# Retention and maxout feed-forward on one core: another order of the first chunks, fewer identity products, weight sums of five units in tile 0

## The chip, the cores and the metric

The kernel runs on one core of a Trainium2 chip. The metric is the device time of one execution in microseconds (us). "Before" and "after" are always timed on the same chip in alternating rounds. A ratio compares the mean times of the two kernels' fast runs in the same rounds, so it isn't quite the ratio of the medians that are quoted.

## The reference

Retention (attention with a decay instead of a softmax), then a feed-forward part with a maximum of three products. All of it is float32; the weights arrive as float64.

```python
B, H, S, D = 8, 8, 576, 64
scores = (q @ k.T) / sqrt(D)              # per batch and head
ret    = scores * gamma[h] ** (i - j)     # for i >= j, else 0
x      = (ret @ v), heads side by side    # 4608 x 512
h      = maximum(maximum(x @ w1, x @ w2), x @ w3)   # 4608 x 768
out    = h @ w_out                        # 4608 x 512
```

## The kernel before

Rows go in 36 chunks of 128 (`g`) and 9 tiles of four chunks (`t`). A chunk has three steps: `transposes` (q and k by identity products on TensorE for the first eight chunks, copied out by ScalarE), `scores` (q times k, mask on VectorE, and the running state), `values` (times v and state, then a multiply into `xT`).

```python
def transposes(g):                       # first eight chunks
    for n, src in (("k", ...), ("q", ...)):
        ... nc.tensor.transpose(pt[:, p, :], pair(src, p), ident[:C, :C])
        nc.scalar.copy(t[:], pt[:])
def scores(g):
    ... nc.tensor.matmul(s[j][:, p, :], lhsT=kT..., rhs=qT...)
    ... nc.vector.tensor_tensor(st[:, j], s[j][:], mask, op=ALU.mult)
    ... nc.tensor.matmul(kv...)
    ... nc.vector.tensor_tensor(t[:], kv[:], states[g][:], op=ALU.add)
        nc.gpsimd.tensor_tensor(t[:], t[:], gs[:], op=ALU.mult)
def values(g):
    ... nc.tensor.matmul(o...)           # st times v, then state times q
    nc.vector.tensor_tensor(xT[t][:, :, i * C:(i + 1) * C], o[:], gq[:], op=ALU.mult)
```

In the traces each engine takes its instructions in the order in which they are written (after the change, for example, ScalarE's copies for chunk 3 come at 23.40 us, behind its steps for the first weight piece, which are written ahead of them). The float64 weights are taken apart by hand, 24 pieces of 128x512; `convert(n)` does the next n of about four steps of a piece. The steps as they fall on the engines (V = VectorE, A = ScalarE, G = GpSimd, which the profile calls DVE, ACT and POOL; there PE is TensorE and PEld its loading of weights):

```python
V expo = high & mask          A mant = low * 2**-52 + 1          # step 1
A expo = relu(...)  V frac = high & 0xFFFFF  A expo = relu(...)  # step 2
V mant = frac * 2**-20 + mant                                    # "whole"
V expo = sign | expo          G w = mant * expo                  # "product"
```

Tile 0 multiplies plainly (`up_plain`, eight matmul records per piece of weights). Later tiles use a scheme of seven smaller products in place of eight (`up`), which needs sums of weight blocks for each of nine units (a unit is one of `w1`, `w2`, `w3` with one of three pairs of column blocks), made once:

```python
def weight_sums(n):
    nc.vector.tensor_tensor(t1, b12, b11, op=ALU.subtract)
    nc.vector.tensor_tensor(t2, b22, t1, op=ALU.subtract)
    nc.gpsimd.tensor_tensor(b12, b22, b12, op=ALU.subtract)
    nc.gpsimd.tensor_tensor(t4, b21, t2, op=ALU.subtract)
```

`sums_of_outs` does the same for the output weights, as small "chores" during `up`. `warm(n)` issues n products of the identity with itself, which count for nothing but keep TensorE busy.

## Time and profile before

| | |
|---|---|
| time | 836.27 us, median of 3 runs (836.2 to 837.62) |
| span of the profile | 834.5 us |
| TensorE busy | 825.3 us |
| first feed-forward product starts | 31.63 us |
| second weight piece used from | 35.13 us |
| pauses of TensorE in tile 1 against its usual step | 0.90 us at 161.63, 0.98 us at 184.25 |

The page, the waits, the chain and the timeline of this kernel are shown and read in the prediction below. In the chain's lines the first number is the start, the second the length (us), then the engine and the source line. In a timeline's lines the bracket tells how long the engine had been idle and what ended it.

### The profile page before, as it was taken

The page shows a single profiled execution, that of the slowest core. Times are in us where ns is not written, and L with a number is a line of the kernel's source. Part 1 is how long each engine was busy: PE and PEld are TensorE (multiplying, and loading weights), DVE is VectorE, ACT ScalarE, POOL GpSimd, SP SyncE. Part 2 cuts the span into 40 slices and gives each one's busy share as a digit, 9 for nine tenths or more (in the row PEclk, how much of TensorE's full clock was granted, in tenths as well). Part 3 has the DMA queues.
Part 4 walks back from the last instruction along what each step waited for, and adds up shares of the span by engine and source line. Part 5 has one row for each costly group of instructions (what it writes and reads, how often), then busy time and mean ns, then how long its engine had stood idle before and what let it go on. Part 6 is the DMA issues. An engine that isn't in the chain of part 4 may idle for free.

```text
span 834.5 us, 12656 instructions
## 1 busy us (share of the span) xinstructions
PE 825.3 (99%) x4636; PEld 671.3 (80%) x4636; DVE 425.9 (51%) x803; ACT 175.1 (21%) x395; POOL 186.9 (22%) x182
## 2 busy tenths in 40 slices
PE   9899999999999999999999999999999999999998
PEld 8555556878888888888888888888888888888887
DVE  2979934774354543554454544544544435433341
ACT  2656721111111101111111111111111011111211
POOL 3435523362211130212011121111111202201000
PEclk9999999999999999999999999999999999999999
DMA  9946521333123322332233313332332224201001
GB/s 225 258 151 188 134 57 42 55 58 75 56 54 57 57 58 58 74 56 56 58 56 67 74 50 55 57 57 81 56 57 54 59 52 79 48 13 38 1 1 50
DMA packets 232509, 59.06 MB, mean 71 GB/s; under 512 B 213504, under 2 KB 230912, under 8 KB 232448
## 3 DMA queue, kind: packets, MB, share of 16 engines
q1 hardware_dynamic: 232304, 58.26, 31.0%
q8 instruction: 36, 0.59, 0.3%
q14 instruction: 25, 0.20, 0.1%
q10 hardware_dynamic: 144, 0.00, 0.0%
HBM read 48.76 MB, written 9.44 MB: 70 GB/s over the span
## 4 chain that ended last, share of the span: by engine, by line
PE 96%; SPq 1%; DVE 1%; DMA 1%; issue 0%; ACT 0%; POOL 0%; POOLq 0%; DVEq 0%
PE x L435 29%; PE z L435 14%; PE dx L311 10%; PE up L493 7%; PE y L435 7%; PE dz L311 5%; PE s L183 5%; PE o L213 4%; PE o L218 4%; PE kv L194 4%; PE dy L311 2%; PE down L484 2%; SPq L146 1%; DMA qraw<-in_q_dram 1%; PE warm L113 1%; PE kt L173 0%
## 5 line engine op out<-in xcount | busy, mean ns | idle before, releaser
L435 PE MATMUL x<-S,T 128*128 128x256 f32 x576 | 147.8, 379 | 0.0
L435 PEld LDWEIGHTS x<-S,T 128*128 128x128 f32 x576 | 109.2, 190 | 15.2
L156 POOL TENSOR_TENSOR vd<-vraw,gk 128x512 f32<-128x512 f32 x36 | 38.8, 1077 | 342.5 <-DMA vraw<-in_v_dram 333.1
L435 PE MATMUL x<-S,w 128*128 128x256 f32 x288 | 74.6, 381 | 1.6 <-DVE h L465 1.6
L435 PE MATMUL x<-xT,w 128*128 128x256 f32 x288 | 74.8, 382 | 0.0
L435 PE MATMUL y<-xT,w 128*128 128x256 f32 x288 | 73.9, 379 | 0.0
L435 PE MATMUL z<-S,w 128*128 128x256 f32 x288 | 73.9, 379 | 0.0
L435 PE MATMUL z<-xT,T 128*128 128x256 f32 x288 | 73.9, 379 | 0.0
L440 ACT COPY p<-x 128x256 f32<-128x256 f32 x72 | 26.8, 373 | 220.5 <-PE x L435 217.8
L465 DVE TENSOR_TENSOR tmp<-x,p 128x256 f32<-128x256 f32 x48 | 20.4, 425 | 103.0 <-PE x L435 103.0
L186 DVE TENSOR_TENSOR st<-s,causal 128x512 f32<-128x512 f32 x72 | 46.3, 685 | 47.9 <-PE s L183 47.9
L493 PE MATMUL up<-xT,w 128*128 128x512 f32 x144 | 63.6, 594 | 2.3 <-DVE xT L220 2.3
L435 PEld LDWEIGHTS x<-S,w 128*128 128x128 f32 x288 | 49.3, 189 | 15.4 <-DVE h L465 2.6
L220 DVE TENSOR_TENSOR xT<-o,gq 128x512 f32<-128x512 f32 x36 | 24.8, 690 | 71.7 <-PE o L218 65.7
L435 PEld LDWEIGHTS y<-xT,w 128*128 128x128 f32 x288 | 54.7, 190 | 7.4
L435 PEld LDWEIGHTS z<-S,w 128*128 128x128 f32 x288 | 54.7, 190 | 7.4
L435 PEld LDWEIGHTS z<-xT,T 128*128 128x128 f32 x288 | 54.0, 189 | 8.2
L435 PEld LDWEIGHTS x<-xT,w 128*128 128x128 f32 x288 | 51.5, 190 | 6.6 <-issue 0.8
L493 PEld LDWEIGHTS up<-xT,w 128*128 128x128 f32 x144 | 26.6, 190 | 32.9 <-issue 29.4
L294 POOL TENSOR_TENSOR H<-h 128x256 f32<-128x256 f32 x24 | 18.8, 784 | 148.2 <-DVE h L478 148.2
L440 ACT COPY u<-x 128x256 f32<-128x256 f32 x72 | 26.8, 373 | 99.9 <-PE x L435 98.5
L454 DVE TENSOR_TENSOR tmp<-y,p 128x256 f32<-128x256 f32 x48 | 20.4, 425 | 51.5 <-PE y L435 51.5
(92 smaller groups left out, 1224.7 us busy)
## 6 DMA issues: line engine op xcount, KB each, us to landing
bits<-in_moe_w_dram SPq DMA_DIRECT2D x18, 512.0 KB, 4.9
out_dram<-osb SPq DMA_DIRECT2D x36, 256.0 KB, 2.1
kraw<-in_k_dram SPq DMA_DIRECT2D x32, 256.0 KB, 3.0
vraw<-in_v_dram SPq DMA_DIRECT2D x32, 256.0 KB, 3.5
qraw<-in_q_dram SPq DMA_DIRECT2D x448, 16.0 KB, 1.8
kxraw<-in_k_dram SPq DMA_DIRECT2D x448, 16.0 KB, 1.8
bits<-in_moe_w_out_dram SPq DMA_DIRECT2D x6, 512.0 KB, 3.4
qraw<-in_q_dram SPq DMA_DIRECT2D x7, 256.0 KB, 4.5
```

Source lines behind the costliest of these rows:

```text
L156: nc.gpsimd.tensor_tensor(t[:], raws.pop(("v", g))[:], gk[:].unsqueeze(2).to_broadcast([C, H, D]), op=ALU.mult)
L183: nc.tensor.matmul(s[j][:, p, :], lhsT=kT[r, p, :], rhs=qT[r, p, :], start=True, stop=True)
L186: nc.vector.tensor_tensor(st[:, j], s[j][:], masks[start_of(g)][:].unsqueeze(1).to_broadcast([C, NP, C]), op=ALU.mult)
L194: nc.tensor.matmul(kv[:, p, :], lhsT=pair(kr, p)[r:], rhs=pair(vds[g], p)[r:], start=True, stop=True)
L213: nc.tensor.matmul(o[D * j:D * (j + 1), p, :], lhsT=vr[:, 2 * p + j, :], rhs=st[:, j, p, :], start=(p == 0), stop=(old == 0 and p == NP - ...
L218: nc.tensor.matmul(o[:, p, :old], lhsT=sd[:, p, :], rhs=qT[:, p, :old], start=False, stop=(p == NP - 1), skip_group_check=True)
L220: nc.vector.tensor_tensor(xT[t][:, :, i * C:(i + 1) * C], o[:], gq[:], op=ALU.mult)
L311: nc.tensor.matmul(out[:, m, :], lhsT=hS[n](fp)[:, m * P:(m + 1) * P], rhs=late["T"][n][:, fp, :], start=first and m == 0 and fp == 0, sto ...
L435: nc.tensor.matmul(out[:], lhsT=w[:, d * P:(d + 1) * P], rhs=xS[t][n][:, d, :], start=first and d == 0, stop=d == 1, skip_group_check=True)
L440: nc.scalar.copy(c[:], src[:])
L454: nc.vector.tensor_tensor(c11, y[:], p1[:], op=ALU.add)
L493: nc.tensor.matmul(ps[:], lhsT=w_sb[i, fb][:, dc * P:(dc + 1) * P], rhs=xT[t][:, dc, :], start=(dc == 0), stop=(dc == NDC - 1))
```

## The change

It lets a chunk's scores follow its own transposes at once, with the next chunk's transposes under the mask, so that TensorE works instead of warming itself. Weight sums move to the last products of tile 0, where VectorE and GpSimd are free, so that less of them crowds tile 1.

```diff
@@ ffn
             else:
+                if t == 1 and n == 0:
+                    sums_of_outs()
                 for _ in up(t, h, fp, i):
                     pass
                 if t == 1:
-                    weight_sums(n + 2)
+                    weight_sums(n + 5)
                 if i == 2:
-                    if t == 1 and fp == 0:
-                        sums_of_outs()
                     sums_of_hidden(h, fp)
@@ ffn, last products of tile 0
                 down(t, h, m)
-                if m >= 2:
-                    weight_sums(m - 2)
+                for n in [[0], [1], [2], [3, 4]][m]:
+                    weight_sums(n)
@@ start
-    warm(9)
+    warm(6)
     ... (loads unchanged)
     decay_values(0)
+    transposes(0)
+    warm(3)
     decay_values(1)
-    transposes(0)
-    warm(5)
+    scores(0)
     transposes(1)
+    values(0)
     decay_values(2)
-    scores(0)
-    values(0)
+    scores(1)
     transposes(2)
+    values(1)
     decay_values(3)
-    scores(1)
+    scores(2)
+    convert(2)
     transposes(3)
-    values(1)
-    scores(2)
-    convert(3)
     values(2)
+    convert(2)
+    scores(3)
     decay_values(4)
-    scores(3)
-    convert(1)
-    transposes(4)
     convert(2)
     values(3)
+    transposes(4)
     convert(4)
```

## The prediction

> **What bounds the kernel now.** I read the page first. Its first part says that TensorE is the engine that counts:
>
> ```profile
> PE 825.3 (99%) x4636; PEld 671.3 (80%) x4636; DVE 425.9 (51%) x803; ACT 175.1 (21%) x395; POOL 186.9 (22%) x182
> ```
>
> Matmul ends are modelled, so 99% could hide short pauses. I therefore compared the starts of neighbouring matmuls in the timeline with the usual step of their kind (a 128x512 one starts 0.43 us after the one before it, a 128x256 one 0.216 us). Between the first product of the feed-forward part (31.63 us) and the end, TensorE keeps that step except at two places. The view of waits for PE names them, together with the late start of the first product:
>
> ```profile
> PE up L493 <- DVE xT L220: 2.3, 1, 2.3
> PE x L435 <- DVE h L465: 1.6, 2, 0.8
> ```
>
> So what can be won without removing matmuls is the time before 31.63 us plus about 1.9 us of pauses (0.90 and 0.98 us against the usual step), at 161.63 and 184.25 us. The removed identity products, the only matmuls that go, lie at the very start.
>
> The start: the chain of waits for the first 40 us, read from its end backward.
>
> ```profile
> 6.95 1.12 PE warm L113 x10
> ...
> 12.28 4.36 DMA qraw<-in_q_dram
> 16.63 0.14 issue
> 16.77 0.63 PE qt L173 x4
> 17.40 1.02 PE o L213 x16
> ...
> 26.33 0.45 PE kt L173 x4
> 26.78 0.68 DVE state L199
> 27.46 0.60 DVE expo L381
> 28.06 1.41 DVE expo L365
> 29.47 1.41 DVE frac L370
> 30.88 0.61 DVE xT L220
> 31.49 0.14 issue
> 31.63 7.21 PE up L493 x16
> ```
>
> Three facts are in it. TensorE waits for the DMA of the fourth chunk's q until 16.63 us. Then it has 12.5 us of its own work: values 1, scores 2, values 2, scores 3, transposes 4, values 3. Last, the multiply into xT (chunk 3) stands behind four VectorE steps, mostly weight conversion, though its matmuls end at about 29.3. The windows give a DMA busy share of 0.84, 0.96 and 0.96 in the first three 10 us. The warm products end at 8.07, long before the DMA wait, so they are off this path.
>
> The rest of the start, from the timeline: the first weight piece is not there before 20.6 us, and VectorE's mask steps, usually 0.42 us, take 1.5 us when POOL is at work.
>
> ```profile
> 20.60 0.77 ACT L366 ACTIVATE mant<-bits,one 128x512 f32<-128x512 uint32 x1 [2.58 <-DMA bits<-in_moe_w_dram]
> ...
> 27.54 1.65 POOL L200 TENSOR_TENSOR state<-state,gs 128x512 f32<-128x512 f32 x1 [0.55 <-DVE state L199]
> 27.98 1.50 DVE L365 TENSOR_SCALAR expo<-bits 128x512 int32<-128x512 int32 x1
> 29.15 1.44 POOL L387 TENSOR_TENSOR w<-mant,expo 128x512 f32<-128x512 f32 x1
> 29.39 1.49 DVE L370 TENSOR_SCALAR frac<-bits 128x512 int32<-128x512 int32 x1
> ```
>
> Each of those two DVE steps ends 0.29 us after the POOL step it met (29.19 and 29.48; 30.59 and 30.88).
>
> **What the Trainium skill says.** "SBUF — State Buffer", section "Who interferes with whom": VectorE and GpSimd share a port pair, held exclusively for a whole instruction; a tensor_scalar in a two-port mode, or a DVE step with two SBUF inputs, waits while GpSimd has it. The trace agrees: the 1.50 us above, and weight sums on DVE that take 0.94 and 0.83 us beside POOL instead of 0.41. "TensorE: Matmul & The Clock Gate", section "What's actually happening": the array runs at half clock until one busy window of about 3.4 us has passed, and an idle window of that length brings it back. Here the warm products start 0.213 us apart, and the record of the granted clock goes from half to full at 6.4 us. "Perfetto Trace Analysis", section "Sequencer Loop": instructions sit in one queue per engine, and each waits for its semaphores. I use this as: a waiting head of a queue holds up everything behind it. The trace agrees (POOL's multiply of v waits 333 us in all for its DMA, and the weight sums queued behind it run only after it).
>
> **The change, part by part.**
>
> *Identity products.* 14 become 9, in records 28 become 18 (each fp32 product is two). That is 10 records of 0.213 us cold, or 0.11 warm: 1.1 to 2.1 us of TensorE. All of it lies before the DMA-paced part: worth 0. The first chunk's products, moved up, keep TensorE busy in their place, so I expect the clock to rise at about 6.4 us again.
>
> *The first chunks' order.* Estimate from durations of the timeline: transposes 0.45 us for each of k and q, scores 1.1, kv 1.1, values 1.0 (+1.1 with state), ACT copies 0.59, masks into st 1.29 per chunk, landings of the inputs as before since the issue order is unchanged. Scores 0 at 6.75, values 0 at 9.9, scores 1 at 10.9, transposes 2 at 13.1 (their inputs land at 12.2 and 13.1), values 1 at 14.0 to 16.1, scores 2 at 16.1 to 18.3, transposes 3 at 18.3, values 2 at 19.2 to 21.3. So far TensorE is 2.8 us ahead of before, where values 2 end and scores 3 start at 24.08. But now the first two conversion steps are written ahead of transposes 3. ScalarE therefore sits on the weight piece until 20.6, then does mant 0.77, expo 0.72, expo 0.72 (to 22.85), and only then the two copies of transposes 3 (to 24.05). Scores 3 start at 24.1, as before, and 2.8 us of the lead are lost in that queue.
> After that: scores and kv 3 to 26.3; st from 25.3 to 26.6; values 3 to 28.7, because transposes 4 (1.0 us) now come after them. On DVE: state 26.6 to 27.25, expo 0.42, then frac, which meets POOL's multiply of the state (27.35 to 28.65) and ends at 28.95. The whole and product steps of piece 0 are already done by 23.6, and its POOL step by 25, so the second meeting of before goes away. xT from 28.95 to 29.6, first product at about 29.7 in place of 31.63: 1.9 us. The second weight piece: whole, expo, frac, product (0.68+0.42+0.42+0.68) from 29.6, plus POOL 1.4: 33.1, and TensorE wants it at 29.7+3.5 = 33.2. It just fits (before: 0.06 us to spare).
> Does the lead survive to the first tile's end? Weight pieces 2 and later are ready 3 us or more before their product, PSUM buffers are free 9 us or more ahead, and VectorE has idle stretches of 0.9, 2.4 and 0.9 us at 47 to 57 us spent waiting for TensorE, so it can follow. Yes.
>
> *Weight sums earlier.* One unit's sums are two DVE steps of 0.42 us and two POOL steps of 0.73 us, 1.8 us on either engine when they meet. Three more units move into the last products of tile 0, where DVE is idle 5.2 us (110.34 to 115.56) and 6.5 us (117.44 to 123.92). Units 0 and 1 go there, and 2, 3, 4 after xT of chunk 7, where two stood: DVE is done with transposes and the first output sums at about 134.5 to 135.5 instead of 131.7; its next need is at 136.02. No new wait. After tile 1's units 0 to 3 follow sums of units 5 to 8; after units 4, 5 and 6 nothing. The two pauses both come from the pile on DVE after the third unit of a triple; for the second:
>
> ```profile
> 179.63 0.94 DVE L414 TENSOR_TENSOR T<-w,w 128x256 f32<-128x256 f32 x1
> ...
> 180.60 0.83 DVE L415 TENSOR_TENSOR T<-w,T 128x256 f32<-128x256 f32 x1
> 181.36 0.70 DVE L167 STREAM_TRANSPOSE kT<-kxraw 128x512 f32<-128x512 f32 x1
> ...
> 183.79 0.41 DVE L465 TENSOR_TENSOR h<-x,p 128x256 f32<-128x256 f32 x1
> ```
>
> Without the two T steps (1.77 us) the step of 183.79 runs some 1.2 us earlier or more, when its matmuls end (about 182.6), and the pause of 0.98 us is gone. The pause of 161.63 stays: the T steps of another unit stand at that place, and the output sums give way to hidden sums of like size. POOL is fuller there (two output sums and two weight sums queue behind the v multiply of 155.57), so it may grow by 0.3. Sum: 0.7 us won.
>
> *Total:* 836.27 - 1.9 - 0.7 = 833.7, rounded to 833.6.
>
> **Rivals.** (a) ScalarE's queue isn't a brake, if the first piece lands sooner or the copies get through: scores 3 at 21.5 and the first product at about 27.5; then weight pieces 0 and 1 become the bound. For it: the new order wants this. Against: the issue order is unchanged and the DMA is 0.96 busy. Time 831.5 to 832.5. (b) A DVE mask step meets POOL once more before xT (+1.4), or the second piece comes 1 us late, as the 0.06 us of before warn. The start then gives 0 to 0.5 and the time is 835.2. (c) Both pauses stay, or the fuller POOL queue makes new ones in tile 1's units 0 to 3: 1 to 2 us lost, time about 835. (d) Both pauses go, as output sums are done by unit 1: 832.7. (e) The clock falls back in TensorE's idle 21.3 to 24.1: 2.8 us is less than one window, and the 2.3 us idle of before did nothing; if so, about +1.
>
> **Range and chances.** Everything that moves lies within 31.6 us of start and 1.9 us of pauses, and the inputs' DMA fixes most of the start. Gains beyond 5 us or losses beyond 2 us need something that I don't see. Three runs before spread 1.4 us (836.2 to 837.62). I take 831.8 to 835.8. A change of 2% is 16.7 us: 0.5% for each side.
>
> **What would show it.** Right: transposes 3 on ACT wait for the first weight piece; scores 3 start near 24; first product at 29.3 to 30.2; no wait at unit 6 of tile 1, one of about 1 us at unit 3; the rest shifted unchanged. Wrong: a first product before 28.5 or after 31, a wait of TensorE between 33 and 134 us, waits in tile 1's units 0 to 2, or a clock that rises later than 7 us.

## The result, and the profile after

The changed kernel took 834.93 us (median of 4 runs, 832.89 to 835.73), the kernel before 836.24 (4 runs, 835.09 to 837.62): ratio 0.998, with an interval of 0.9957 to 1.0003, so these runs alone don't tell it from no change. The time is inside the predicted range, 1.3 us above the predicted 833.6. The profile was taken in the slowest of the four executions (835.73 us, span 834.0), so it shows a bad case, as the experiments make plain.

The page of the changed kernel, first part (busy us, share of the span, number of records):

```profile
PE 823.8 (99%) x4626; PEld 670.5 (80%) x4626; DVE 427.3 (51%) x803; ACT 174.7 (21%) x395; POOL 186.7 (22%) x182
```

The ten records of identity products are gone and TensorE is busy for 1.5 us less. Its waits (total us, times, longest us):

```profile
PE s L183 <- ACT qT L175: 2.0, 1, 2.0
...
PE up L493 <- POOL w L387: 1.4, 1, 1.4
PE x L435 <- DVE h L465: 1.2, 1, 1.2
```

One of the two pauses in tile 1 is left and has grown: against the usual step it is 1.34 us, at 162.03 us. The wait for xT is gone; in its place are a wait of the scores for ScalarE and one of the feed-forward part for a weight piece. The chain of waits at the start shows both:

```profile
14.57 5.89 DMA bits<-in_moe_w_dram
20.46 0.02 issue
20.49 1.41 DVE expo L365
...
21.92 0.73 ACT expo L368
...
22.68 0.72 ACT expo L371
23.40 0.47 ACT kT L175
23.87 0.49 ACT qT L175
...
24.41 1.21 PE s L183 x16
...
32.05 2.94 POOL w L387
34.99 0.04 issue
35.03 3.70 PE up L493 x8
```

The first weight piece lands at 20.46 us; ScalarE works on it; then come the copies of chunk 3 and its scores at 24.41. The piece's first step on VectorE takes 1.41 us where 0.42 is usual; POOL's multiply of the state runs beside it, from 20.32 to 21.60. The first feed-forward product starts at 30.00 us (before: 31.63). The lead is 1.6 us there, but the second weight piece is ready only at 34.98 us, and the second product starts at 35.03 where it started at 35.13 before. Of 1.6 us, 0.1 is left. POOL shows why. Its record for that piece is 2.93 us long (2.94 in the chain), where one such multiply alone is 1.27 (the kernel before, in its profile: 1.65). The timeline of the kernel before at its second piece (one line), then that of the changed kernel (the POOL line merges two multiplies):

```profile
33.43 1.65 POOL L387 TENSOR_TENSOR w<-mant,expo 128x512 f32<-128x512 f32 x1 [2.84 <-DVE expo L381]
```
```profile
31.88 0.69 DVE L376 SCALAR_TENSOR_TENSOR mant<-frac,mant 128x512 f32<-128x512 int32 x1
32.05 4.16 POOL L387 TENSOR_TENSOR w<-mant,expo 128x512 f32<-128x512 f32 x2 [1.92 <-DVE expo L381]
32.48 0.43 DVE L365 TENSOR_SCALAR expo<-bits 128x512 int32<-128x512 int32 x1
32.81 0.43 DVE L370 TENSOR_SCALAR frac<-bits 128x512 int32<-128x512 int32 x1
33.15 0.69 DVE L381 SCALAR_TENSOR_TENSOR expo<-bits,expo 128x512 int32<-128x512 int32 x1
```

POOL's multiply starts at 32.05, just after a VectorE step. VectorE goes on with three more without a gap, until 33.84, and POOL ends at 34.98, 1.1 us after that and 1.27 us after 33.71. So it seems to have waited through nearly four VectorE steps in a row and only then had the port pair that the two engines share ("SBUF — State Buffer" of the Trainium skill, section "Who interferes with whom").

From 35 to 134 us nothing in TensorE's steps differs between the two kernels, and the shift of 0.1 us stays. Tile 1 gives 0.5 us (0.98 gone, 0.90 grown to 1.34). The sum, 0.6 us, is close to the difference of the two profiles' spans (834.5 and 834.0). But the four times lie up to 2.8 us apart, so something at the start must differ from execution to execution. That was the first thing to test.

### The profile page after: what moved, and what is told of

It is laid out like the page before. It is cut to its first block, busy times and chain, and to the rows that moved or that the text cites. A ratio compares the mean times of both kernels' runs of the same rounds, so it can differ in the third digit from the quotient of the medians.

```text
span 834.0 us, 12632 instructions
## 1 busy us (share of the span) xinstructions
PE 823.8 (99%) x4626; PEld 670.5 (80%) x4626; DVE 427.3 (51%) x803; ACT 174.7 (21%) x395; POOL 186.7 (22%) x182
## 4 chain that ended last, share of the span: by engine, by line
PE 95%; DMA 2%; DVE 1%; SPq 1%; ACT 0%; POOL 0%; issue 0%; DVEq 0%
PE x L435 30%; PE z L435 15%; PE dx L311 10%; PE y L435 7%; PE up L493 7%; PE dz L311 5%; PE s L183 4%; PE o L213 4%; PE o L218 4%; PE kv L194 4%; PE dy L311 2%; PE down L484 2%; SPq L152 1%; DMA bits<-in_moe_w_dram 1%; DMA gs<-in_state_decay_dram 1%; SPq L146 1%
## 5 line engine op out<-in xcount | busy, mean ns | idle before, releaser
L183 PEld LDWEIGHTS s<-qT,kT 64*128 64x128 f32 x576 | 35.0, 187 | 15.6 <-issue 11.7
```

Of the source, the lines that this page charges most:

```text
L183: nc.tensor.matmul(s[j][:, p, :], lhsT=kT[r, p, :], rhs=qT[r, p, :], start=True, stop=True)
```

## The experiments

Theory A: the landing of the first weight piece paces the start through ScalarE's queue, and a race between POOL and VectorE at the second piece gives back up to 1.5 us of it. Rivals: the spread lies elsewhere (matmul rate, DMA, clock), or the order alone decides. Twelve kernels ran in three groups of four, five rounds each, each group on another chip. The kernel before had medians of 837.52, 837.79 and 837.22 us in the three groups, so kernels of different groups are compared by their ratios to it.

| run | median us | ratio to before (95% interval) | first, second product start in its profile, us |
|---|---|---|---|
| group 1: changed again | 834.69 | 0.9968 (0.9951 to 0.9986) | 28.07, 31.81 |
| new start only | 834.26 | 0.9971 (0.9952 to 0.9990) | 30.25, 33.99 |
| weight sums only | 836.64 | 0.9995 (0.9978 to 1.0012) | 31.66, 36.87 |
| second piece on VectorE | 833.24 | 0.9953 (0.9936 to 0.9970) | 29.51, 33.01 |
| group 2: before, filled | 836.58 | 0.9985 (0.9973 to 0.9998) | 31.81, 35.32 |
| changed, filled | 833.81 | 0.9952 (0.9939 to 0.9966) | 29.50, 34.55 |
| copies first | 832.32 | 0.9939 (0.9927 to 0.9951) | 28.51, 33.55 |
| skip the third unit | 833.03 | 0.9945 (0.9931 to 0.9958) | 29.99, 33.77 |
| group 3: fourteen products | 835.67 | 0.9968 (0.9952 to 0.9984) | 30.85, 35.89 |
| three edits | 830.86 | 0.9921 (0.9908 to 0.9934) | 28.22, 31.72 |
| masks first | 832.05 | 0.9933 (0.9919 to 0.9946) | 28.89, 33.16 |
| weight first | 831.41 | 0.9926 (0.9912 to 0.9939) | 28.25, 31.76 |

### The changed kernel once more

No edit.

> The changed kernel itself, once more. Theory A (in the first profile POOL lost the shared port four times in a row while it formed the second weight piece, and the second feed-forward product began at 35.03 instead of 33.4 us): executions differ by whether POOL loses that race, so the median is 0.5 to 2.2 us under before, the first product starts at 29.7 to 30.3 us in this profile too, and the second anywhere from 33.4 to 35.1. Rival B (the spread lies elsewhere, in matmul rate or DMA): the second product starts at 35.0 again, and the time is 0.5 us under before; the spread shows as a shift that grows along the whole span.

The ratio is 0.9968, or 2.7 us of the 837.5, against 0.998 in the first runs, and here the interval lies clear of 1. The profile is of a good execution (832.3 us). Two things are better in it than in the first one. The first weight piece lands at 19.22 us (20.46 in the first profile), so scores 3 start at 22.48 and the first product at 28.07. And POOL gets the port at the second piece after one VectorE step; the timeline of this run:

```profile
30.11 1.65 POOL L387 TENSOR_TENSOR w<-mant,expo 128x512 f32<-128x512 f32 x1 [1.90 <-DVE expo L381]
30.56 1.49 DVE L365 TENSOR_SCALAR expo<-bits 128x512 int32<-128x512 int32 x1
```

This time it is VectorE that waits, 1.49 us for a step of 0.42. The second product starts at 31.81, 3.74 us after the first; in the first profile it was 5.04 us after. The pause at the fourth unit of tile 1 is 1.17 us. The expectation had the first product between 29.7 and 30.3, which was too narrow: the DMA's landing moves too. Its Rival B fails: the second product did not start at 35.0 again, and the difference lies at the start.

In the seven profiles that have the changed order with ScalarE on the first piece before chunk 3's copies (the changed kernel twice, new start only, second piece on VectorE, changed and filled, skip the third unit, fourteen products), the first product starts 8.8 to 9.6 us after that piece lands, over landings from 19.22 to 22.02 us. Its start follows the landing, as Theory A says. The second product starts at 31.81 to 35.89 us in the six of them that leave the second piece to POOL, 34.2 on average, against 35.13 and 35.32 in the two profiles of the old start without a fall of the clock (see below): about 1.0 us earlier.

### Each half alone

New start only: the hunks in `ffn` undone. Weight sums only: the start's hunk undone.

```diff
 # new start only, against the changed kernel
-                    weight_sums(n + 5)
+                    weight_sums(n + 2)
 ... (sums_of_outs after the third unit, weight_sums(m - 2) after products 2 and 3 of tile 0)
```
```diff
 # weight sums only, against the changed kernel
-    warm(6)
+    warm(9)
 ... (the start in the order of before)
```

> The new order of the first chunks and the nine identity products, with the weight sums as before. Theory A: first product at 30.0 us, second at 33.4 to 35.1, the two pauses near 161 and 184 us stay (0.9 and 1.0 us): 0.1 to 1.7 us faster than before. Rival B: the order itself is worth its 1.6 us in every execution, as another first product's end hides the second piece: 1.6 us faster.

> The weight sums as changed, with the order of the first chunks and fourteen identity products as before. Theory A: first product at 31.6 us, second at 35.1, the pause after the fourth unit of tile 1 grows to 1.3 us and the one after the seventh is gone: 0.5 us faster than before. Rival C: without the new start the two pauses both go or both stay: 1.9 us faster, or 0.

The new start alone is worth 0.29% (2.4 us), the sums alone 0.05% (0.4 us, interval across 1), together 0.34% against 0.32% for the whole. Within these intervals the halves add up. In the profile of the new start the two pauses stay at 0.84 and 0.97 us. In that of the sums the seventh unit's pause is gone and the fourth's stays at 0.90, so it has not grown there. (Five of the six runs of the sums alone have the slowdown told of next, against seven of the eleven of before, so their 0.4 us may be too low.)

The profile of the sums alone shows something that no theory had. The second product comes 5.2 us after the first, although its weight piece is ready at 35.12, as before. The windows of that run (start and end, length, busy us of PE, PEld, DVE, ACT and POOL with counts, then the granted clock as a share of full speed, DMA share, GB/s):

```profile
30.00:33.00 3.00, 1.34 (x3) 0.71 (x4) 3.00 (x6) 2.15 (x4) 0.63 (x1) 0.95 0.66 233
33.00:37.00 4.00, 4.00 (x7) 1.63 (x6) 3.34 (x5) 0.93 (x2) 2.23 (x2) 0.61 0.60 174
```

The granted clock is 0.61 in the second window. The record of the clock has it at half from 32.7 to 36.1 us, for 3.4 us, and the second product starts 1.7 us later than it does after a first product in full clock (5.2 against 3.5 us). Ahead of it TensorE stood idle from 29.3 to 31.66, the wait for xT that the kernel before has too.

Why here and not in the profile of before? The clock records of the packed traces tell. In the run of the sums alone the clock rises to full at 5.40 us and falls at 32.71, eight times 3.413 us later. Counted in stretches of 3.413 us from the rise, the 14 profiles hold 15 falls (this one, and one in each after its last matmul), and every one comes at the end of a stretch. Each of these 15 stretches had 2.23 us or more without a matmul (this one 2.31); none of the other 3373 had over 1.89. In the profile of before the rise is at 6.40 us, so a stretch ends at 30.29: the same wait of 2.3 us is split into 0.98 and 1.33 us, and no fall follows. So in these traces a wait of this length costs again only when it falls almost whole into one stretch.

Each run's mean clock, which doesn't count the time before the first rise (it is 1.000 in the profile of before), tells whether such a fall took place ahead of the last matmul: 3.4 us at half speed is 0.2% of the span. The fall after the last matmul takes up to 0.1% (0.999 in five of the profiles), so I count a fall at 0.998 or less. Of the 31 runs of the kernel before in the three groups, 19 are at 0.998 or 0.997. Their medians are 837.95, 838.08 and 838.34 us, and those of the other 12 runs 835.5, 836.9 and 836.6. The changed kernel has three such runs of six in group 1 (834.9 to 835.1, the rest 832.3 to 834.5), and none of its first four. This became Theory D.

### Second weight piece on VectorE

```diff
-            nc.gpsimd.tensor_tensor(w, mant[:], expo[:].bitcast(FP32), op=ALU.mult)
+            engine = nc.vector if piece == pieces[1] else nc.gpsimd
+            engine.tensor_tensor(w, mant[:], expo[:].bitcast(FP32), op=ALU.mult)
```

> The changed kernel, but the multiply that forms the second weight piece is done by VectorE (0.68 us, estimate from its like) instead of POOL, so POOL has nothing to fetch through the shared port there. Theory A: the second piece is ready near 32.6 us, the second product starts at 33.4, no wait, and the whole is 1.5 us under the first profile of the changed kernel (span about 832.5), with less spread. Rival B (something else holds the second product, such as the queue of DVE or the landing of a piece): it starts at 34.5 or later again and the time doesn't move by over 0.3 us.

The piece is ready at 32.19 us and the second product starts 3.51 us after the first, which is its own length: no wait is left. The step in the timeline of this run:

```profile
31.50 0.69 DVE L388 TENSOR_TENSOR w<-mant,expo 128x512 f32<-128x512 f32 x1
```

The median is 1.4 us under the changed kernel's on the same chip (833.24 against 834.69), though the two intervals overlap. Only one run of six has a fall of the clock. That POOL's part, and not the landing or VectorE's queue, held the second product is shown by the profile; that POOL waited for the port is read from the times of its record, and no run isolates it.

### Filling TensorE's idle time

```diff
 # kernel before
     values(3)
+    warm(8)
     convert(4)
```
```diff
 # changed kernel
     convert(2)
+    warm(6)
     scores(3)
```

> The kernel before, with eight identity products more (16 records, 1.8 us at 0.112 us, an estimate from the warm ones of the profile of before) in TensorE's idle time of 2.3 us ahead of the first feed-forward product. Theory D (the granted clock falls to half for one window of 3.4 us, as in the profile of the sums alone from 32.7 us, when TensorE stands idle for most of a window; each fall costs 1.7 us): the runs with a mean clock of 0.998 or less, 7 of 11 for the kernel before, nearly vanish, and the median comes to 835.2, some 2 us under before. Rival E (falls are the chip's own, whatever TensorE does): the same share of runs at 0.998, and the time of before.

> The changed kernel, with six identity products (1.35 us) in TensorE's idle time before the scores of chunk 3. Theory D: no or hardly any run at 0.998, so the slow ones (834.9 to 835.1) go: median 832.5 to 834.0, against 834.7; what remains of spread is POOL's wait at the second weight piece. Rival E: half of the runs at 0.998 as before, median 834.7.

Work that counts for nothing makes the kernel before faster: ratio 0.9985, 836.58 against 837.79 us. None of its five runs is at 0.998 or less (five of nine of the kernel before in the same rounds are), and its median is 0.3 us under that of the unfallen runs of before on this chip (836.9). The expected 835.2 was taken from another chip's runs and missed. The changed kernel filled has no fall in five runs either. Its profile shows the lost race at the second piece again (5.04 us between the products), and it stays at 834 to 835 in two runs. Five runs each are few, but the whole record bears Theory D out. The profiles of the kernel before, the sums alone, the changed kernel, the new start only, second piece on VectorE, skip the third unit and fourteen products all show a wait of TensorE of 2.0 us or more between 8 and 32 us (but for the second one of the changed kernel, 0.7), and 33 of the 70 runs of these kernels that have a clock on record show a fall. In the other six kernels (the two filled ones, copies first, three edits, masks first and weight first) the longest wait there is 1.2 us, and none of 30 runs has a fall. What spread remains in the changed kernel I put down to the race and the landing. Only one fall ahead of the last matmul was ever profiled; that the other 0.998 runs have theirs at TensorE's wait of the start is inferred from these counts.

### Copies of chunk 3 first

```diff
-    convert(2)
     transposes(3)
+    convert(2)
```

> The changed kernel, with the transposes of chunk 3 written ahead of the first two conversion steps, so that their copies on ScalarE don't wait for the first weight piece. Theory A: scores 3 start at 21.5 in place of 24.4, but their masks on VectorE now queue behind the steps of the first piece (until about 24.3), so the first product comes at 28.7 (1.3 us earlier), and the second at 32.2 to 33.7. With TensorE's pause moved after the scores; 0.5 to 1.5 us faster than the changed kernel. Rival (ScalarE's queue is all that held it): first product at 27.2, 2.8 us earlier. Rival (second weight piece is the bound): first product earlier, the second at 35.0 all the same, no gain.

Scores 3 start at 21.94 us and the first product at 28.51, close to what Theory A expects. This run's first piece landed as late as 21.25, and the changed order would have given 30.0 or later (8.8 us after it). The median is 832.32; the ratio is 0.29% better than the changed kernel's in group 1, part of it because none of the five runs has a fall. But now the masks wait behind the first piece's steps on VectorE: in the chain of waits, the product step of the first piece ends at 24.20 and the masks follow. The race at the second piece was lost here as well, with 5.04 us between the products.

### No weight sums after the third unit

```diff
-                    weight_sums(n + 5)
+                    weight_sums({0: 5, 1: 6, 3: 7, 4: 8}.get(n, len(units)))
```

> The changed kernel, with the weight sums of units 5 to 8 after units 0, 1, 3 and 4 of tile 1 instead of 0, 1, 2 and 3, so none stand between the third unit's maxima and the fourth unit. Theory A (the two T steps on VectorE, 1.77 us, make the pause at the fourth unit): the pause of 1.2 to 1.3 us is gone or under 0.2 us, and nothing new at the seventh unit: 1.2 us faster than the changed kernel. Rival (POOL's queue behind the late multiply of v makes it, through the shared port): it stays at 0.6 us or more.

Both pauses are gone; TensorE keeps its step all through tile 1. VectorE reaches the step that the fourth unit waits for with time to spare, in the timeline of this run:

```profile
158.83 0.42 DVE L465 TENSOR_TENSOR h<-x,p 128x256 f32<-128x256 f32 x1 [0.62 <-PE x L435]
```

It had been idle 0.62 us and waited for TensorE, not the other way. POOL, though the edit takes two of its steps away here as well, still works without a gap from its multiply of v at 153.95 us to 163.27, so that rival falls. The ratio is 0.9945 against 0.9968 in group 1: 0.23%, with intervals that overlap. The pause, 0.91 to 1.39 us in the profiles with the changed sums and the new start, is worth some 0.14%.

### Fourteen identity products

```diff
-    warm(6)
+    warm(9)
 ...
-    warm(3)
+    warm(5)
```

> The changed kernel with all fourteen identity products back (nine, then five). Theory A: the first scores start about 0.9 us later, but the scores of chunk 1 wait for the state decay's DMA (landing at 10.1 to 11.1 us) and those of chunk 3 for the first weight piece, so it is caught up: first product at 28.0 to 30.3 as in the changed kernel's profiles, time within 0.5 us of 834.7 to 834.9. Rival (fewer identity products are worth their 1.1 to 2.1 us): first product 1 to 2 us later and the time by as much longer.

The ratio is 0.9968, the same as with nine. With intervals of 1.4 us to either side the times alone could not exclude the rival's 1.1 us; the profile does. In it scores 0 start at 8.29 us instead of 7.17, scores 1 at 12.37 instead of 11.99, and scores 3 at 25.26, which is 3.24 us after the first piece's landing (22.02 in this run), as in the good run with nine (3.26). So 1.1 us at chunk 0 is 0.4 at chunk 1 and nothing at chunk 3. The removed products were worth nothing by themselves. The expected bound of 30.3 us for the first product missed (30.85), because the piece landed later than in any other profile.

### Three edits at once

Copies first, second piece on VectorE, and no sums after the third unit, as shown above.

> The changed kernel with three edits at once: the copies of chunk 3 first, the second weight piece formed on VectorE, and the sums skipped after the third unit. If their causes are separate, the gains add: first product at 28.5, second at 32.0, no pause in tile 1: 1.3 to 1.5 us (start), 1.2 (POOL's lost races, in about half of the executions), 1.2 (pause): median 831.0, against 834.7. If they share a cause, it comes to 832.0 or more, as the copies first alone (832.3).

The gains add: 830.86 us, ratio 0.9921, the best, 6.4 us under the kernel before on the same chip. Its five runs lie within 1.5 us, none has a fall of the clock (seven of the eleven of before on this chip have one, so a part of the gain is that). In the profile the products start at 28.22 and 31.72 us, and these are all the waits of TensorE that the view lists:

```profile
PE warm L113 <- POOL ident masks.py:199: 1.4, 1, 1.4
PE o L213 <- DVE st L186: 0.6, 2, 0.4
```

The first is the wait for the identity at the very start, the second the masks of chunk 3.

### Masks of chunk 3 first

```diff
     transposes(3)
     convert(2)
     values(2)
-    convert(2)
     scores(3)
-    decay_values(4)
-    convert(2)
+    convert(2)
     values(3)
+    decay_values(4)
+    convert(2)
     transposes(4)
     convert(4)
```

> As the three edits, and the scores and masks of chunk 3 are written ahead of the last two steps of the first weight piece, and values 3 ahead of the second piece's first two steps. Theory A (in the copies-first kernel VectorE's queue took over from ScalarE's, as the wait of values 3 for st shows): first product at 27.6, second at 31.1: 0.9 us faster than the three edits, median 830.1. Rival: the first weight piece on POOL is now late (27.5 or more) and the second still later, so no gain.

Slower than the three edits by 1.2 us (832.05 against 830.86, same chip). The rival had it. The masks do come earlier, but the last VectorE step of the first piece then meets POOL's multiply of the state. The chain of waits of this run:

```profile
24.56 0.66 DVE state L199
25.22 0.60 DVE mant L376
25.82 1.68 DVE expo L381
```

That step takes 1.68 us where 0.60 is usual, the first piece is ready at 28.84 us and the first product starts at 28.89, the second 4.3 us later. The wait moved from the masks to the weights.

### First weight piece before chunk 3

```diff
-    load(3)
-    load_weights(2)
+    load_weights(1)
+    load(3)
+    load_weights(1)
```

with the changed order of chunks, the second piece on VectorE and no sums after the third unit.

> The changed order of the first chunks, with the first weight piece loaded before chunk 3's inputs, the second piece formed on VectorE and the sums skipped after the third unit. Theory A (the landing of the first weight piece paces the start through the queue of ScalarE): that piece lands near 17.5, scores 3 start at 21.5 as soon as values 2 end, first product at 26.5 to 27.5, second 3.5 later: median about 830.0. Rival: chunk 3's inputs now come 2.5 us later and hold scores 3 at 23 or later: no gain over the three edits.

The piece lands at 17.00 us, the inputs of chunk 3 at 17.9 to 19.8, but scores 3 start only at 22.67: VectorE takes the piece up at 19.8, after the mask and state of chunk 2, and ScalarE's two steps and copies follow to 22.6. The products start at 28.25 and 31.76, within 0.04 us of the three edits, and the times agree (831.41 and 830.86, intervals overlap). Once the landing no longer paces the start, the queue of VectorE does. The expected 0.9 us more was not there.

## Why the prediction was right or wrong

The time was right: 834.93 us against 833.6 with a range of 831.8 to 835.8, and "within 2%" was never in doubt. In the first runs the medians differ by 1.3 us, half of the predicted 2.6 (the prediction's own sum is 833.67 us; it states 833.6). The larger sample gives 2.7, but that agreement is luck in part, as the points show: on average the second product comes some 1.0 us earlier, where the prediction carried 1.9 us on from the start.

- *Identity products worth nothing:* right, shown by the run with fourteen.
- *ScalarE's queue behind the first weight piece, scores 3 at 24.1, first product at 29.7:* right. Measured 24.41 and 30.00 in the first profile, and shown by the copies-first run. What the working missed is that the landing it took from the profile of before (20.6 us) varies, 19.22 to 22.02 us over the profiles with the new order, and the first product with it (28.07 to 30.85).
- *TensorE's lead of 2.8 us ahead of that queue:* too large, without effect. Values 2 end at 22.39 us in the first profile and not at 21.3, since scores 1 start at 11.99 instead of 10.9: scores 0 came 0.4 us later, and scores 1 then waited 0.7 us for VectorE's first state step, which had waited for the DMA of the state decay until 11.15.
- *"It just fits":* this is the step that failed. The prediction gave POOL 1.4 us for the second piece, for 33.1 us (its own terms add up to 33.2, the very moment at which TensorE wants the piece). Its profile of before had 1.65 us for that multiply. POOL took 2.93 us in the first profile, as it seems to have waited through nearly four VectorE steps, and the second product came 1.5 us after the end of the first. It took 2.92 to 2.93 us in four of the seven profiles that leave this multiply to POOL under a new start, and 1.65 in the other three; even there the second product is some 0.25 us late. The rival (b) named the place ("the second piece comes 1 us late").
- *The lead survives to the end of tile 0:* right, whatever lead there was at the second product. No wait of TensorE between it and 134 us.
- *No new wait from the moved sums, pause at the seventh unit gone:* right in all profiles with the new sums.
- *Pause at the fourth unit stays and may grow by 0.3:* right in kind. It was 0.90 us before, and 0.90 (sums alone) to 1.39 us in the seven profiles with the changed sums that keep the step. Its cause, the two VectorE steps of the weight sums, is shown by the run that skips them.
- *The clock:* the statement in rival (e), that the 2.3 us idle of before did nothing, was true of the one profile and wrong of the kernel. 19 of its 31 runs in the three groups have a lower mean clock and take 1.2 to 2.4 us more. The prediction asked whether a gap is as long as a whole window; in these traces 2.23 us without a matmul in one stretch of 3.413 were enough. The new start may make this rarer (none of 4 and 3 of 6 for the changed kernel), a gain that the prediction didn't count.
- *The signs of being right and wrong:* in the first profile the signs of "right" came true, but so did one of "wrong": TensorE waited 1.4 us for the second piece at 35.03 us, between 33 and 134. In the second profile two more did, a first product before 28.5 us (28.07) and a clock that rises after 7 us (7.17; 7.00 in the first, 6.4 expected), and that was the fastest run. The rise lies anywhere from 4.8 to 7.5 us in the 14 profiles and says little about the time.

How much of the 2.7 us is clock and how much is order can't be told exactly, but most is order. In group 1 the changed kernel is 3.0 us ahead both among fallen runs (834.95 against 837.95, medians) and among the others (832.48 against 835.52); the difference in the share of fallen runs (3 of 6 against 7 of 11) is worth some 0.3 us, an estimate from these counts.

## What to carry to other kernels

Where TensorE is saturated, look at the few microseconds before it becomes so: what comes first in the queue of a helper engine decides, and a step that waits for a DMA should not be written ahead of short copies that TensorE needs. Give a deadline on GpSimd beside a busy VectorE at least one lost race of slack (here 1.7 us: 2.93 instead of 1.27), or put that one step on VectorE. And when a kernel's times spread by 0.3% on one chip, read the mean granted clock of each run before comparing medians: an idle gap ahead of the dense part can cost twice (here 2.3 us of idle time, then 1.7 us by a halved clock). Filling it removed the second cost, closing it both.

## What the Trainium skill lacked or had wrong

- "SBUF — State Buffer", section "Who interferes with whom", says that the second engine to issue blocks until the first finishes. It doesn't say that a blocked GpSimd instruction can be passed over by the VectorE instructions that come after: here POOL's multiply of 1.27 us took 2.93 us while four VectorE steps ran back to back, and 1.65 us in executions in which it seems to have got the port after the first. That it was passed over is read from these times; no run isolates it.
- "TensorE: Matmul & The Clock Gate", section "What's actually happening", has the clock drop after an idle window of about 3.4 us. It doesn't say how much of a window must be idle. Here the clock fell to half for 3.4 us after TensorE was idle for 2.3 us, with matmuls on both sides: of the stretches of 3.413 us counted from the rise, all 15 with 2.23 us or more without a matmul ended in a fall, and none of the 3373 with 1.89 or less. In 19 of 31 runs of the kernel before the mean clock fits such a fall (0.998 or less), for 1.2 to 2.4 us each.
- No page that I read says how far the landing of a DMA behind some 3.5 MB of queued inputs (14 transfers of 256 KB) moves from run to run. Here the first weight piece, always issued in the same order, landed between 19.22 and 22.02 us.
